# Writing out the order of all five engine queues in a scan, gated MLP and mixture-of-experts kernel

## Chip, core and metric

The kernel runs on one core of one Trainium2 chip. The metric is the device time of one execution in microseconds (us); the time before is the median of three runs.

The core has a matrix engine (PE, whose weight loads the profile lists apart as PEld), a vector engine (DVE), an activation engine (ACT), a general engine (POOL) and a queue engine (SP) that issues the loads. Each works through its own list of instructions in order, and waits where an instruction needs a result of another engine.

## The reference, cut to what matters

Three stages run one after the other. All inputs are float32 when drawn; the two matrices of the second stage reach the kernel as 64-bit floats.

```python
# 1. scan: 4 x 8 heads, 768 positions, head width 32, state 16
L = np.exp(cum[..., :, None] - cum[..., None, :]) * causal
y_intra = (C @ B.T * L) @ x
y_inter = (C @ state) * np.exp(cum)
state = decay * state + (B * decay_from_j).T @ x
# 2. MLP over x of 3072 tokens x 256
h = x @ w_in                                   # 256 -> 2048
x = (h * (1 / (1 + np.exp(-1.702 * h)))) @ w_out   # 2048 -> 256
# 3. eight experts, one for each token
expert_idx = np.argmax(normalised(x) @ normalised(expert_emb).T / tau, axis=1)
out[mask] = gate_w[mask, None] * (np.maximum(x[mask] @ w1[e], 0.0) @ w2[e])   # 256 -> 1024 -> 256
```

## The kernel before, in words

**Tiles and groups.** The 3072 tokens are 24 tiles of 128, and three tiles make a group of 384 (`TPG`, `NG` = 8). The scan handles a tile as two chunks of 64 positions, in four stages: `ssm_a` (lines 282 to 294) scales x into `xtb` on POOL; `ssm_c` (311 to 338) makes the state update `pU` on PE, and on DVE the carried state `T` and its decayed copy `S`; `ssm_b` (296 to 309) makes the score matrix `pS` on PE and masks it into `mt` on DVE; `ssm_d` (340 to 371) makes `pY` on PE from `mt` and `S`, scales it on DVE (`ye`), and splits it into a high part on ACT (`yh`) and a low part on POOL (`yl`). Two heads lie side by side in a matmul, with zeros kept in `c4b` and `xtb` where heads must not mix.

**MLP blocks.** A block (g, f) takes a group g through one of 16 slices f of the hidden width: `gemm1` (line 440) makes six matmuls of 384 columns into `ph`, ACT applies the gate twice (445, 446), DVE forms the low part (447), and `gemm2` (456), two blocks later, makes nine matmuls of 256 columns. There are 128 blocks. Groups 0 and 1 make the first pass together (32 blocks), groups 2 to 7 one pass each. The first pass also decodes the weights: `decode_w` (254 to 275) turns each of 16 slices of 64-bit words into two 32-bit parts, with three ACT operations, three on DVE (266, 268, 272) and two on POOL (270, 275). A block needs its slice decoded.

**Experts.** After a group's pass its tokens are routed (`route0` to `route3`; the expert products are 24 DVE operations at line 515 for groups 0 to 5, and go through PE transposes for 6 and 7) and scattered by expert into `slots`. Ten expert units then run the third stage (`egemm1`, line 657, and `egemm2`, 683).

**What sets the order.** Up to the expert units only SP's queue is in the written order; the program is also written in some order for the other engines, but there a scheduler chooses, instruction by instruction, which ready one comes next. From the expert units on, all are in written order. The loads go out by the table `LOADS`: three buffers hold scan inputs, `c4b` is refilled in place, and the edge factors `ee` come back from memory after a round trip through `ebuf`. An instruction at the head of SP's queue that waits for a buffer holds up every load behind it.

```python
SEQ = ("t0 t1 t2 t3 t4 t5 d0 d1 d2 d3", "")
LOADS = ("s0 c0 s1 s2 w0", "c1 e0 e1", "s3 w1", "s4 w2", "s5 w3", "", "", "")
MENG = {mybir.EngineType.SP}
    man.enter_context(tc.manual_schedule(engines=MENG))
```

Of the kernel before, what the change touches and what calls it, by code (L numbers as in the profile page):

```python
# [24 lines left out]
P = 128  # L25
# [11 lines left out]
DLEAD = 4  # L37
GDOT = 6
NXT = 2
LAG = 1  # L40
TSW = 6
SEQ = ("t0 t1 t2 t3 t4 t5 d0 d1 d2 d3", "")
EORD = (1, 0)
XV = ((), ())
YV = ()
LV = ()
LOADS = ("s0 c0 s1 s2 w0", "c1 e0 e1", "s3 w1", "s4 w2", "s5 w3", "", "", "")
FH = 4
MENG = {mybir.EngineType.SP}
SOFF = (1, 2, 3, 4)  # L50
ROFF = (8, 9, 4, 5)
# [8 lines left out]
SB2, SBT, SX = 256, 256, 256  # L60
SSMW = SB2 + SBT + SX

K_TRI, K_SEL, K_MASK, K_ID, K_RANK, K_ONE, K_W8, K_EB, K_E8, K_PK, K_NK, K_BK, K_CAP, K_END = (
    0, 128, 160, 224, 352, 480, 608, 616, 624, 632, 640, 664, 688, 696)
NBLK = 24


def host_constants():
# [16 lines left out]
    c[:, K_CAP:K_CAP + NE] = CAPS  # L85
    tok = (np.arange(NTILE)[None, :] * P + i[:, None]).astype(np.int32)
# [3 lines left out]
def host_layout(x, a, B, C):  # L90
# [16 lines left out]
    ct = C.reshape(NB, NH, TPB, P, NS).transpose(0, 2, 1, 4, 3).reshape(NTILE, P, P)  # L107
    at = a.reshape(NB, 2, 4, TPB // TPG, TPG, P).transpose(5, 0, 3, 2, 4, 1).reshape(P, -1)
# [15 lines left out]
def body(ctx, tc, ssm, ct, aall, cst, tok, wcat, emb, tau, w1, w2, out):  # L124
# [20 lines left out]

    NGB = 4
# [14 lines left out]
    man.enter_context(tc.manual_schedule(engines=MENG))  # L161
# [8 lines left out]

    warm = const.tile([P, 1], F32, name="warm")
# [3 lines left out]
    c4b = [sp.tile([P, NPAIR, TPG, P], F32, tag=f"c4{i}", name=f"c4b{i}", bufs=1) for i in range(2)]  # L175
    xtb = [sp.tile([P, 2, NPAIR, 2, HD], F32, tag=f"xt{i}", name=f"xtb{i}", bufs=1) for i in range(NXT)]
    nc.vector.memset(c4b[0], 0.0)
    for xt in xtb:
        nc.gpsimd.memset(xt, 0.0)
    nc.vector.memset(c4b[1], 0.0)  # L180

    raw_s, c4_s, ee_s = {}, {}, {}

    def load_c4(g):
        c4_s[g] = c4b[g % 2]
        for p in range(NPAIR):
            h = slice(32 * p, 32 * p + 32)
            nc.sync.dma_start(out=c4_s[g][h, p, :, :],
                              in_=ct[g * TPG:(g + 1) * TPG, h, :].rearrange("t p c -> p t c"))
# [8 lines left out]
    def load_ssm(t):  # L198
        r = sp.tile([P, SSMW], F32, tag="raw", name=f"raw{t}", bufs=3)
        nc.sync.dma_start(out=r, in_=ssm[t])  # L200
        raw_s[t] = r

# [6 lines left out]
    loads = {"s": load_ssm, "c": load_c4, "e": load_ee, "w": load_w}  # L209

    def load(names):
        for n in names.split():
            loads[n[0]](int(n[1:]))

    load(LOADS[0])
# [824 lines left out]
```

## Time and profile before

| | |
|---|---|
| median of three runs | 604.48 us (604.26 to 604.73) |
| the profiled execution | 605.19 us |
| its span, first to last instruction | 603.4 us |
| mean granted clock of PE | 0.97 of full speed |
| busy | PE 553.6 us (92%), DVE 352.1 (58%), ACT 249.6 (41%), POOL 180.2 (30%) |
| on the chain that ended last | PE 68%, issue 9%, DVE 9%, DMA 7%, ACT 3% |

The profiled execution is 0.7 us above the median, and 1.8 us of its time lie outside the span. A share over the whole span is a mean over stages with different limits, so the stages are read apart. PE's records are pipelined: two records that follow each other overlap, and what one costs is read from start to start, not from its own length. A float32 matmul of the scan is recorded as two passes, a matmul of the MLP or the experts as one.

### The profile page before, as it was taken

What the parts mean: (1) busy time and instruction counts of PE and PEld (TensorE: products, weight loads), DVE (VectorE), ACT (ScalarE), POOL (GpSimd) and SP (SyncE); (2) the same over time, 40 slices, a digit from 0 to 9 for tenths busy, and PEclk for the clock granted to TensorE, in tenths of its full rate; (3) what the DMA queues carried; (4) which work ended last, traced back from release to release, by engine and by line L of the source; (5) the groups of instructions that cost most, each with busy time, mean ns of one, the idle gap of its engine ahead of it and who ended that gap; (6) DMA issues with size and microseconds to landing.
All of it is one profiled execution on the core that took longest, in us unless ns stands there. A gap on an engine that the chain in (4) does not pass through costs nothing.

```text
span 603.4 us, 11521 instructions
## 1 busy us (share of the span) xinstructions
PE 553.6 (92%) x4318; PEld 510.4 (85%) x4318; DVE 352.1 (58%) x1019; ACT 249.6 (41%) x578; POOL 180.2 (30%) x204
## 2 busy tenths in 40 slices
PE   5487678999999999999999999998999999999992
PEld 3256568899899889999898999997999999999992
DVE  3284699723796862863762862446576865545330
ACT  3152566533533433433433433448355445445220
POOL 4382588700113421122222202039221102211111
PEclk9688888999999999999999999999999999999996
DMA  6616769401003112011101000057146534231000
GB/s 193 168 66 172 252 211 276 136 27 54 1 2 93 53 36 81 30 36 55 57 7 48 2 1 28 2 167 266 66 150 212 186 117 153 101 106 45 25 25 24
DMA packets 32759, 56.27 MB, mean 93 GB/s; under 512 B 3306, under 2 KB 22592, under 8 KB 32576
## 3 DMA queue, kind: packets, MB, share of 16 engines
q1 hardware_dynamic: 30208, 49.22, 26.7%
q0 software_dynamic: 2496, 6.32, 2.9%
q8 instruction: 34, 0.56, 0.4%
q14 instruction: 21, 0.17, 0.1%
HBM read 44.87 MB, written 11.01 MB: 93 GB/s over the span
## 4 chain that ended last, share of the span: by engine, by line
PE 68%; issue 9%; DVE 9%; DMA 7%; ACT 3%; POOL 1%; SPq 1%; POOLq 0%; ACTq 0%; DVEq 0%
PE ph L440 20%; PE po L456 16%; PE qo L683 9%; PE qh L657 9%; PE po_a L456 3%; PE pS L304 3%; PE pY L350 2%; DMA raw<-in_ssm 2%; DMA wraw<-in_wcat 2%; PE pY L358 2%; PE pU L318 2%; POOL out L129 1%; DVE u L266 1%; DVE glb L447 1%; DVE S L331 1%
## 5 line engine op out<-in xcount | busy, mean ns | idle before, releaser
L440 PE MATMUL ph<-yh,dw 128*128 128x384 f32 x512 | 164.4, 362 | 10.6 <-DVE glb L447 8.7
L445 ACT ACTIVATE ghb<-ph 128x384 fp32r<-128x384 f32 x128 | 62.8, 491 | 172.4 <-PE ph L440 171.0
L447 DVE TENSOR_TENSOR glb<-ph,ghb 128x384 fp32r<-128x384 f32 x128 | 70.9, 554 | 104.0 <-ACT ph L446 101.5
L440 PEld LDWEIGHTS ph<-yh,dw 128*128 128x128 f32 x512 | 95.8, 191 | 19.9 <-DVE glb L447 11.1
L456 PE MATMUL po<-dw,ghb 128*128 128x256 f32 x576 | 104.0, 286 | 1.4 <-ACT ghb L445 1.4
L440 PE MATMUL ph<-yl,dw 128*128 128x384 f32 x256 | 87.1, 340 | 0.0
L456 PEld LDWEIGHTS po<-dw,ghb 128*128 128x128 f32 x576 | 84.2, 189 | 2.9 <-ACT ghb L445 1.6
L456 PE MATMUL po<-dw,glb 128*128 128x256 f32 x288 | 68.7, 282 | 1.1 <-DVE glb L447 1.1
L129 POOL DMA_INDIRECT out<-ob,xs x29 | 29.2, 1006 | 127.2 <-DVE ob L694 121.2
L290 POOL TENSOR_TENSOR xtb<-raw,einv 64x256 f32<-64x256 f32 x48 | 33.3, 694 | 104.5 <-PE pY L350 61.4
L446 ACT ACTIVATE ph<-ph 128x384 f32<-128x384 f32 x128 | 62.5, 488 | 0.0
L664 DVE SCALAR_TENSOR_TENSOR glb<-qh,ghb 128x256 fp32r<-128x256 f32 (+5 forms) x72 | 36.4, 507 | 41.8 <-ACT ghb L663 38.5
L515 DVE SCALAR_TENSOR_TENSOR pr<-xr,enb 128x256 f32<-128x256 f32 x144 | 59.3, 451 | 0.1
L683 PE MATMUL qo<-weh,ghb 128*128 128x256 f32 x208 | 58.6, 282 | 0.0
L683 PE MATMUL qo<-wel,ghb 128*128 128x256 f32 x208 | 58.5, 281 | 0.0
L683 PE MATMUL qo<-weh,glb 128*128 128x256 f32 x208 | 58.5, 281 | 0.0
L663 ACT ACTIVATE ghb<-qh 128x256 fp32r<-128x256 f32 (+5 forms) x72 | 32.5, 452 | 61.6 <-PE qh L657 57.8
L657 PE MATMUL qh<-xh,weh 128*128 128x256 f32 (+5 forms) x160 | 53.3, 333 | 1.8 <-DVE glb L664 1.1
L657 PE MATMUL qh<-xl,weh 128*128 128x256 f32 (+5 forms) x160 | 51.4, 321 | 0.1
L657 PE MATMUL qh<-xh,wel 128*128 128x256 f32 (+5 forms) x160 | 51.2, 320 | 0.0
L456 PEld LDWEIGHTS po<-dw,glb 128*128 128x128 f32 x288 | 49.1, 188 | 1.4 <-DVE glb L447 1.3
L440 PEld LDWEIGHTS ph<-yl,dw 128*128 128x128 f32 x256 | 49.3, 193 | 0.3
(179 smaller groups left out, 1016.9 us busy)
## 6 DMA issues: line engine op xcount, KB each, us to landing
wer<-in_w SPq DMA_DIRECT2D x32, 512.0 KB, 3.6
raw<-in_ssm SPq DMA_DIRECT2D x24, 384.0 KB, 3.0
wraw<-in_wcat SPq DMA_DIRECT2D x16, 512.0 KB, 4.2
slots<-padr SPq DMA_DIRECT2D x8, 516.0 KB, 11.1
ee<-ebuf SPq DMA_DIRECT2D x8, 384.0 KB
xs<-slots SPq DMA_DIRECT2D x3, 516.0 KB
c4b<-in_ct SPq DMA_DIRECT2D x32, 48.0 KB, 4.3
xs<-slots SPq DMA_DIRECT2D x3, 387.0 KB, 3.2
```

The source lines that it names most:

```text
L129: i = nc.gpsimd.indirect_dma_start(in_offset=None, oob_is_err=False, **kw)
L290: eng.tensor_tensor(out=xt[hs, :, :, h, :].rearrange("p c q d -> p (c q) d"), in0=r[hs, SB2 + SBT:].rearrange("p (c d) -> p c d", d=HD), i ...
L440: nc.tensor.matmul(ph, lhsT=wslice(w, f, k * P, k * P + P), rhs=y[g][:, k, :], start=(n == 0), stop=(n == 5))
L445: nc.scalar.activation(out=a[:, :GT], in_=ph, func=AF.Gelu_apprx_sigmoid)
L446: nc.scalar.activation(out=ph, in_=ph, func=AF.Gelu_apprx_sigmoid)
L447: nc.vector.tensor_tensor(out=c[:, :GT], in0=ph, in1=a[:, :GT].bitcast(F32), op=ALU.subtract)
L456: nc.tensor.matmul(po[g][tl], lhsT=l, rhs=r, start=(f == 0 and i == 0 and (off + tl) % 2 == 0), stop=(f == NF - 1 and i == 2), skip_group_ ...
L515: nc.vector.scalar_tensor_tensor(out=pr, in0=xr[:, tl, :D], scalar=1.0, in1=enb[:, e, :], op0=ALU.mult, op1=ALU.mult, accum_out=ld[:, tl, ...
L657: nc.tensor.matmul(ph[:, :n], lhsT=w[:, o:o + P], rhs=x[u][:, k, :n], start=(i == 0), stop=(i == 5))
L663: nc.scalar.activation(out=a[:, :n], in_=ph[:, :n], func=AF.Relu)
L664: nc.vector.scalar_tensor_tensor(out=c[:, :n], in0=ph[:, :n], scalar=0.0, in1=a[:, :n].bitcast(F32), op0=ALU.max, op1=ALU.subtract)
L683: nc.tensor.matmul(qacc(u, s), lhsT=l, rhs=r, start=(f == 0 and i == 0 and (s % 2 == 0 or ss is not None)), stop=(f == NFE - 1 and i == 2) ...
```

## The change

It does five things.

1. All engines are in written order from the start. The start and the first pass follow the string `START`, in which a letter is one operation (on one engine, or one run on PE) and the number the tile, weight slice or block: A scales x, U, S and Y are PE runs of the scan, T, M, E, s, H and L its steps on DVE, ACT and POOL; R, u, p, v, h and l are the steps of `decode_w`; G, g, c and O are `gemm1`, the gate, the low part and `gemm2`; N and W are loads. The later passes are lists of jobs with a block number each.
2. The scan's matmuls no longer carry zeros for the other head: they use 32 or 64 rows and 32 output columns at a place of their own in PE's array. A tile has 8 (U), 4 (S) and up to 32 (Y) matmuls where it had 8, 2, 8 and 4. In the later passes U and S stand together as one run, and Y is a second run two blocks later. DVE makes the carried state in one operation instead of two, and the decayed copies move to ACT (four small operations a tile). POOL scales x in one operation instead of two.
3. Scan inputs have six buffers instead of three, C comes with them (512 KB a tile) and `c4b` with its loads is gone. Groups 0 and 1 take their edge factors from PE (24 small matmuls a group) instead of through memory. Six tiles and five weight slices are asked for at the start.
4. The first two weight slices have their low part made on DVE instead of POOL.
5. Routing is spread over a pass: DVE operations two or three to a block, the rest in steps; group 1 is routed through PE instead of with 24 DVE operations. The order of the experts is settled after six groups instead of seven, and the first experts' weights are loaded and split from block 4 of the last pass.

The core of the diff:

```diff
-SEQ = ("t0 t1 t2 t3 t4 t5 d0 d1 d2 d3", "")
-LOADS = ("s0 c0 s1 s2 w0", "c1 e0 e1", "s3 w1", "s4 w2", "s5 w3", "", "", "")
+PEG = (1, 6, 7)
+NXT = 3
+START = (
+    "A0 X0 A1 U0 A2 x0 T0 S0 s0 U1 M0 R0 u0 S1 Y0 T1 W5 p0 M1 s1 U2 E0 S2 A3 T2 H0 Y1 r4 R1 u1 U3 E1 L0 s2 W6 r0 "
+    "M2 p1 H1 T3 Y2 s3 v0 S3 E2 L1 R2 M3 X1 A4 h0 u2 H2 U4 x1 l0 S4 W7 N6 N7 N8 T4 p2 Y3 M4 s4 v1 E3 L2 h1 Y4 H3 "
+    "v2 R3 l1 G0 E4 A5 h2 L3 U5 g0 T5 S5 l2 H4 G1 c0 s5 M5 L4 g1 Y5 u3 R4 O0 c1 W8 p3 E5 G2 H5 v3 O1 r1 g2 L5 h3 "
...
-    man.enter_context(tc.manual_schedule(engines=MENG))
+    man.enter_context(tc.manual_schedule(engines={mybir.EngineType.SP, mybir.EngineType.PE, mybir.EngineType.DVE,
+                                                  mybir.EngineType.Activation, mybir.EngineType.Pool}))
...
-        r = sp.tile([P, SSMW], F32, tag="raw", name=f"raw{t}", bufs=3)
+        r = sp.tile([P, SSMW], F32, tag="raw", name=f"raw{t}", bufs=6)
...
+    for t in range(3):
+        load_ssm(t)
+    load_w(0)
+    load_ssm(3)
+    load_w(1)
+    load_ssm(4)
+    load_ssm(5)
+    for f in (2, 3, 4):
+        load_w(f)
...
     def ssm_b(t):
...
         for c in range(2):
-            nc.tensor.matmul(ps[:, c * 256:(c + 1) * 256], lhsT=r[:, c * P:(c + 1) * P],
-                             rhs=c4_s[g][:, :, tl, c * Q:(c + 1) * Q], start=True, stop=True)
+            for w in range(2):
+                h = slice(64 * w, 64 * w + 64)
+                nc.tensor.matmul(ps[:, w, c * P:(c + 1) * P].rearrange("p (k i) -> p k i", k=2),
+                                 lhsT=r[h, c * P:(c + 1) * P], rhs=cpad(t)[h, :, c, :],
+                                 start=(c == 0), stop=True, skip_group_check=True)
...
+    def ssm_state(t):
...
+                nc.vector.scalar_tensor_tensor(out=T, in0=old, scalar=dec[:, i:i + 1], in1=u, op0=ALU.mult, op1=ALU.add)
...
+    def ssm_pads(t):
+        for s1, old, i in st[t]["pads"]:
+            for r in range(2):
+                nc.scalar.mul(out=s1[:, r, :], in_=old, mul=decm[:, i, r:r + 1])
...
     def ssm_d(t):
...
+        def place(k, q, r, c):
+            o = 32 * (2 * q + (k ^ r))
+            return py[o:o + 32, r, c * Q:(c + 1) * Q]
+
+        heads = [(k, q, r) for q in range(2) for k in range(2) for r in range(2)]
         for c in range(2):
...
+            for k, q, r in heads:
+                h = slice(64 * r, 64 * r + 64)
+                nc.tensor.matmul(place(k, q, r, c), lhsT=xt[h, c, 2 * k + q, :], rhs=mt[h, k, c, q, :],
+                                 start=(c == 0), stop=True, skip_group_check=True)
...
+            for k, q, r in heads:
+                h = slice(32 * (2 * k + q), 32 * (2 * k + q) + 32)
+                nc.tensor.matmul(place(k, q, r, c), lhsT=sps[c][h, r, :], rhs=cpad(t)[h, q, c, :],
+                                 start=False, stop=True, skip_group_check=True)
...
+    seq0 = [(0, f) for f in range(LEAD)] + [(1, 0)]
+    for f in range(1, NF):
+        seq0 += [(1, f)] + ([(0, f + LEAD - 1)] if f + LEAD - 1 < NF else [])
...
+    def tile_steps(jobs, t0, at):
+        for i, k in enumerate(at):
+            for d, w in ((0, "U"), (0, "T"), (2, "Y"), (3, "E")):
+                jobs.append((k + d, lambda t=t0 + i, w=w: step(t, w)))
```

SP's queue at the start, before (`raw` is a tile's scan input, `wraw` a weight slice):

```order
L166 DMA al<-in_aall 128x576
L167 DMA kc<-in_cst 128x696
L200 DMA raw_111<-in_ssm 128x768
L188 DMA c4b_103<-in_ct 32x3x128 x4
L207 DMA wraw_121<-in_wcat 128x512
L229 DMA ebuf<-et 96x2x128
L188 DMA c4b_104<-in_ct 32x3x128 x4
L194 DMA ee_155<-ebuf 128x1x768
L200 DMA raw_198<-in_ssm 128x768
L207 DMA wraw_200<-in_wcat 128x512
```

and now:

```order
L184 DMA al<-in_aall 128x576
L185 DMA kc<-in_cst 128x698
L207 DMA raw_112<-in_ssm 128x1024
L217 DMA wraw_118<-in_wcat 128x512
L207 DMA raw_120<-in_ssm 128x1024
L217 DMA wraw_122<-in_wcat 128x512
L217 DMA wraw_302<-in_wcat 128x512
L286 DMA ebuf<-et 96x2x128
```

The write of `et` and the reads of `ebuf`, which wait for ACT and for each other, stood ahead of the fourth tile and the second weight slice; now twelve loads stand ahead of the write (of those alike, some are left out in both lists), and the first read of `ebuf` comes later still.

DVE's queue, now, from the first tile's state to what the first MLP block waits for (`u` and `v` are steps of the decode, `dw` its result):

```order
L395 COPY T_0_236<-pU_224 128x32
L369 TENSOR_TENSOR mt_257<-pS_241,kc 128x512
L316 TENSOR_SCALAR u_263<-wraw_118 128x512
L318 SCALAR_TENSOR_TENSOR u_263<-wraw_118,u_263 128x512
L403 SCALAR_TENSOR_TENSOR T_0_297<-T_1_239,dec,pU_248 128x32
L444 TENSOR_TENSOR ye_322<-pY_271,ee_234 128x256
L327 SCALAR_TENSOR_TENSOR v_451<-ab_261,u_263 128x512
L336 TENSOR_TENSOR dw_0_173<-v_451,dw_0_169 128x512
L369 TENSOR_TENSOR mt_563<-pS_510,kc 128x512
```

Steps of tiles and of weight slices alternate; rows of the same kinds between these are left out. The first three slices' `u` stand ahead of the first block now, where the second stood behind a load that came late.

PE's queue in a later pass, one tile, before (each row but the last two with some sixteen MLP matmuls behind it):

```order
L318 MATMUL pU_1496<-xtb_106,raw_1438 32x64 x2
L318 MATMUL pU_1496<-xtb_106,raw_1438 32x64 x6
L350 MATMUL pY_1582<-mt_1553,xtb_106 64x64 x4
L358 MATMUL pY_1582<-c4b_104,S_0_1505 64x2x64 x2
L358 MATMUL pY_1582<-c4b_104,S_1_1509 64x2x64 x2
```

and now, with two blocks between the second row and the third:

```order
L381 MATMUL pU_1763<-xtb_109,raw_1539 32x32 x8
L361 MATMUL pS_1772<-raw_1539 128x128 x4
L426 MATMUL pY_1852<-mt_1787,xtb_109 32x64 x16
L433 MATMUL pY_1852<-raw_1539,S_0_1777 32x64 x8
L433 MATMUL pY_1852<-raw_1539,S_1_1780 32x64 x8
```

The six pieces of a tile (the score matrix and a second piece of L350 stand elsewhere in the list of before) have become two, and the matmuls of a tile 44 instead of 22.

## Rows read from the trace of the kernel before

**Rows 1.** Busy time by stage: us, then PE, PEld, DVE, ACT, POOL, clock, DMA.

```profile
0.00:60.00 60.00, 39.12 (x346) 29.23 (x347) 29.83 (x62) 20.01 (x39) 27.48 (x46) 0.86 0.55 149
60.00:112.00 52.00, 41.05 (x315) 36.27 (x313) 46.13 (x63) 31.18 (x62) 37.95 (x30) 0.90 0.81 240
112.00:158.10 46.10, 44.49 (x338) 41.36 (x338) 19.09 (x48) 18.71 (x47) 9.42 (x12) 1.00 0.14 44
158.10:419.80 261.70, 258.52 (x2072) 238.16 (x2073) 159.09 (x626) 105.99 (x268) 69.72 (x84) 1.00 0.16 53
419.80:603.40 183.60, 170.40 (x1253) 165.41 (x1251) 97.92 (x223) 73.74 (x163) 35.65 (x35) 0.98 0.31 103
```

**Rows 2.** The chain that ended last, in order of time: start, us, what.

```profile
14.01 14.33 DMA raw<-in_ssm
...
52.78 12.11 DMA wraw<-in_wcat
```

**Rows 3.** PE's timeline, one block with nothing between: start, us, line and matmul.

```profile
397.90 0.34 PE L440 MATMUL ph<-yh,dw 128*128 128x384 f32 x1
...
398.94 0.28 PE L456 MATMUL po<-dw,glb 128*128 128x256 f32 x1
...
400.01 0.34 PE L440 MATMUL ph<-yh,dw 128*128 128x384 f32 x1
```

**Rows 4.** Groups of matmuls between 158.1 and 419.8 us: count, busy us, mean ns.

```profile
L440 PE MATMUL ph<-yh,dw 128*128 128x384 f32 x368 | 116.4, 357 | 1.4 <-DVE glb L447 1.4
L456 PE MATMUL po<-dw,ghb 128*128 128x256 f32 x576 | 104.0, 286 | 1.4 <-ACT ghb L445 1.4
...
L318 PE MATMUL pU<-xtb,raw 128*32 128x64 f32 x192 | 10.6, 230 | 0.0
```

**Rows 5.** PE's timeline where parts of the scan stand between blocks.

```profile
17.76 0.43 PE L318 MATMUL pU<-xtb,raw 128*32 128x64 f32 x16
18.12 0.44 PE L358 MATMUL pY<-c4b,S 128*64 128x128 f32 x4
...
120.38 0.44 PE L440 MATMUL ph<-yh,dw 128*128 128x384 f32 x1
...
122.69 0.45 PE L350 MATMUL pY<-mt,xtb 128*64 128x64 f32 x8
123.07 0.44 PE L440 MATMUL ph<-yh,dw 128*128 128x384 f32 x1
...
136.06 1.02 PE L304 MATMUL pS<-c4b,raw 128*128 128x256 f32 x4
136.73 0.53 PE L440 MATMUL ph<-yh,dw 128*128 128x384 f32 x1
```

**Rows 6.** Weight loads of line 318: count, shortest, median and longest ns.

```profile
L318 PEld LDWEIGHTS pU<-xtb,raw x384: 106/109/178, 11.9 to 349.1; 128*32 128x32 f32 x192
```

**Rows 7.** The first step of the decode on DVE: as rows 6, first and last start.

```profile
L266 DVE TENSOR_SCALAR u<-wraw x16: 415/575/1559, 12.4 to 109.2; 128x512 int32<-128x512 int32 x16
```

**Rows 8.** Groups by line over the whole span: count, busy us, mean ns, idle before.

```profile
L447 DVE TENSOR_TENSOR glb<-ph,ghb 128x384 fp32r<-128x384 f32 x128 | 70.9, 554 | 104.0 <-ACT ph L446 101.5 <-ACT ghb L445 1.8 <-issue 0.2
...
L270 POOL TENSOR_TENSOR u<-u,rd 128x512 int32<-128x512 int32 x16 | 23.2, 1452 | 11.0 <-DVE u L268 8.5 <-ACT rd L264 2.4
...
L272 DVE SCALAR_TENSOR_TENSOR v<-ab,u 128x512 f32<-128x512 f32 x16 | 17.8, 1111 | 0.0
...
L307 DVE TENSOR_TENSOR mt<-pS,kc 128x512 f32<-128x512 f32 x24 | 16.5, 686 | 6.2 <-PE pS L304 5.8 <-issue 0.4
L268 DVE SCALAR_TENSOR_TENSOR u<-wraw,u 128x512 int32<-128x512 int32 x16 | 15.1, 946 | 0.2
L266 DVE TENSOR_SCALAR u<-wraw 128x512 int32<-128x512 int32 x16 | 13.2, 822 | 20.0 <-DMA wraw<-in_wcat 19.7
...
L364 DVE TENSOR_TENSOR ye<-pY,ee 128x256 f32<-128x256 f32 x24 | 10.0, 417 | 7.6 <-DMA ee<-ebuf 4.3 <-PE pY L358 2.4 <-POOL yl L369 0.6
...
L336 DVE TENSOR_TENSOR T<-pU,S 128x64 f32<-128x64 f32 x40 | 8.7, 218 | 1.7 <-PE pU L318 1.3
```

More of the change, by code (lines that the diff above doesn't have):

```diff
@@ L173, in body @@
     nc.scalar.activation(out=warm, in_=warm, func=AF.Ln)
[L175 to L189, printed above, removed]
+    xtb = [sp.tile([P, 2, NPAIR, HD], F32, tag=f"xt{i}", name=f"xtb{i}", bufs=1) for i in range(NXT)]
+    raw_s, ee_s = {}, {}
     def load_ee(g):
@@ L426, in prefill, with router3 @@
+    def router3():
+        pen = pss.tile([P, 512], F32, tag="m", name="pen")
+        for k in range(2):
+            nc.tensor.transpose(pen[:, k * NE:(k + 1) * NE], em[:, k * P:(k + 1) * P], ident[:NE, :NE])
+        nc.vector.tensor_copy(out=ent.rearrange("p k e -> p (k e)"), in_=pen[:, :2 * NE])
     def prefill(e):
@@ L434, in gemm1 @@
     def gemm1(g, f):
[L435 removed]
+        pf = hbank()
         ph = pf[:, :GT]
@@ L722, in rows_of, with early_rows @@
         return rreg[k]
+    early_base = const.tile([P, NE], F32, name="early_base")
+    def early_rows():
+        nc.vector.tensor_tensor(out=base, in0=base, in1=early_base, op=ALU.max)
     def expert_order():
@@ L839, in body, with tile_loads @@
+    for n in START.split():
+        fns[n[0]](int(n[1:]))
+    def tile_steps(jobs, t0, at):
+        for i, k in enumerate(at):
+            for d, w in ((0, "U"), (0, "T"), (2, "Y"), (3, "E")):
+                jobs.append((k + d, lambda t=t0 + i, w=w: step(t, w)))
+    def tile_loads(jobs, t0, at):
+        for i in range(TPG):
+            jobs.append((at + 2 * i, lambda t=t0 + i: load_ssm(t)))
+    order, first = expert_order(), set()
     for pi, gs in enumerate(passes):
         jobs = []
-        nxt = passes[pi + 1] if pi + 1 < len(passes) else ()
@@ L868, in body @@
+        if gn < NG:
+            tile_steps(jobs, TPG * gn, (2, 6, 10))
+        if gn + 1 < NG:
+            tile_loads(jobs, TPG * (gn + 1), 7)
+            jobs += [(13, lambda t=TPG * (gn + 1) + i: step(t, "A")) for i in range(TPG)]
+            jobs.append((14, lambda: load_ee(gn + 1)))
         if pi + 1 == len(passes):
@@ L887, in body @@
                 po[gs[0]] = [pts[0][:, :D], pts[0][:, D:], pts[1][:, :D]]
-            for i, g in enumerate(gs):
-                lag = LAG * i
-                for ff in range(f - lag if f >= lag else NF, f - lag + 1 if f < NF - 1 else NF):
-                    block(g, ff)
-            for ff, fn in jobs:
-                if ff == f:
+            block(g, ff)
+            for k, fn in jobs:
+                if k == f and fn in first:
+                    fn()
+            low_part()
+            for k, fn in jobs:
+                if k == f and fn not in first:
                     fn()
@@ L954, in body @@
         finish(NU - 1, [s])
-    hand.close()
     man.close()
```

460 lines of the change are left out of this document (249 added, 211 removed), and 8 rows, old and new, of the table START.

## The prediction, made before the changed kernel was run

> **What bounds the kernel now.** I read the stages first, because the share of PE over the whole span hides them. From 158.1 to 419.8 us PE is busy for 258.5 of 261.7 us at a granted clock of 1.00, and the experts behind it keep PE at 170.4 of 183.6 [rows 1]: there PE is the bound, and only less work on PE can help. The two stages ahead of 112 us are different. PE is busy for 39.1 of 60 and 41.1 of 52 us there, at 0.86 and 0.90 of its clock [rows 1], and in the second DVE is busy for 46.1 of 52. The chain of waits says what came last: a scan load of 14.3 us and then a weight load of 12.1 us [rows 2]. These are loads that were issued late, behind others on SP's queue; DVE stood idle for 19.7 us before the decode's first step with a weight load as the releaser [rows 8]. After the second load DVE had the decode of the remaining slices in front of it, all at once. So the start is bound by loads, then by DVE, and everything behind it by PE.
>
> **Prices.** A block without anything between takes 1.04 us for its six matmuls and 1.07 us for its nine, 2.11 us from start to start [rows 3]. A run of scan passes in the middle costs more than its passes: a block with eight passes of line 350 inside takes 2.69 us (120.38 to 123.07), 0.58 more, while these passes themselves take 0.38 (122.69 to 123.07) [rows 5]. So changing from MLP matmuls to scan and back costs about 0.2 us each time.
>
> **Scan tiles in the later passes.** Of the 258.5 busy microseconds, 368/4 = 92 runs of six matmuls (95.7 us) and 576/6 = 96 runs of nine (102.7) are MLP [rows 1, 4], which leaves 60 for 192/16 = 12 tiles [rows 4] and the routing. Priced by the timeline, a tile's `pU` takes 0.36 us, `pS` 0.67 (136.06 to 136.73), its sixteen passes of line 350 twice 0.38 [rows 5]; its eight of line 358, twice as wide, I put at 0.8, and six switches at 1.2. That is 3.8, or 46 for twelve, and with slowed neighbours (which I can't part from routing) somewhat over 4 each; the rest, some 7 to 10 us, is routing.
>
> After the change a tile is two runs (0.4 us of switches). `pU` has the same sixteen passes: 0.36. `pS` has eight passes of half the width where four took 0.67: 0.4 to 0.8, and I keep 0.67. `pY` is the uncertain term: 32 matmuls, 64 passes of 64 columns into 32 array columns each. The nearest row is `pU`, whose passes also go to 32 array columns and stream 64 columns: sixteen in 0.36 us, 22.5 ns each. The other end is line 350, whose passes take 64 array columns: 0.38/8 = 47 ns [rows 5]. That makes 1.44 to 3.0 us. I take `pU`'s, because what is alike is the placing, and get 0.36 + 0.67 + 1.44 + 0.4 = **2.9 us** a tile, with 2.6 to 4.6 as the ends. DVE's state operations of 218 ns [rows 8] are halved; their copies go to ACT, which is busy for 106 of 261.7 us [rows 1], and hide there.
>
> **The start.** With the loads asked for up front, DVE has work from 12.4 us, when the first weight slice is there [rows 7]. The new queue puts onto DVE, ahead of what the first block needs: three `u` steps (3 × (0.822 + 0.946) = 5.3), eight state operations (8 × 0.22 = 1.8), four masks (4 × 0.69 = 2.7), three `ye` (3 × 0.42 = 1.25), one `v` (1.11) [rows 8], and the first low part, for which I take the mask's 0.69 as the same size of tile. Together 12.9 us, so 25.3; then `Y4` on PE and its hand-over, 2 to 3 us. First block at about **28 us**.
>
> **The first pass.** Each of 16 slices brings two blocks and a quarter of a tile (tiles 5 to 8). PE: 2 × 2.11 + 2.9/4 = 4.95 us. DVE: 0.822 + 0.946 + 1.111 for the decode, two `glb` of 0.554, and a quarter of a tile's two state operations, mask and `ye`, (2 × 0.218 + 0.686 + 0.417)/4 = 0.39: 4.4 us [rows 8]. PE is the longer, but the two hand work to each other many times per slice and neither may now overtake; I add 5% and take 5.2. 16 × 5.2 = 83, so the first pass ends at 28 + 83 = **111 us**, with two groups through the MLP and nine tiles scanned.
>
> **The rest.** 96 blocks × 2.11 = 202.6; 15 tiles × 2.9 = 43.5; routing 9 (the 7 above and 2 for group 1, now on PE); idle 3, as now [rows 1]. That is 258, so the experts begin at 369 and not at 419.8. They and the tail are unchanged: 183.6 [rows 1]. Span 369 + 184 = 553; with the 1.8 us outside the span 555, against 605.2 of the profiled execution. The execution stands 0.7 above the median, so 554.5: I say **555 us**, some 50 less, of which about 33 come from the start and 17 from the tiles.
>
> **Set to nothing, with the cover.** The larger scan loads (512 KB a tile) go through DMA engines that are busy 0.81 at the most now and 0.16 later [rows 1]; if they came late again, the stall of 12 to 14 us [rows 2] would be back. ACT's added copies lie beside 31.2 busy of 52 us [rows 1]. The 24 edge matmuls a group, 48 passes at 22.5 ns and more, are a little over 1 us where PE waits for DVE anyway. The low parts moved to DVE for two slices are in the sum above once; the second costs 0.7 of DVE's slack. Later loads pass nothing that blocks on SP's queue, since six buffers replace three.
>
> **Rival 1: DVE and POOL get in each other's way.** The first decode step took from 415 to 1559 ns for one shape, median 575 [rows 7], and POOL's step of the same decode takes 1452 ns [rows 8]: the slow ones are as long as if DVE stood still for one operation of POOL. If in the tight first pass all three decode steps last 1.56, DVE needs 3 × 1.56 + 2 × 0.554 + 0.39 = 6.2 us a slice, 16 × 6.2 = 99, the pass ends at 127 and the kernel at **571**. For it: POOL has almost 3 us of decode per slice, two steps of that size. Against: my means already hold the mixture, much of it from a stage with POOL busy for 38 of 52 us [rows 1]. Chance 0.18. [...]
>
> **Rival 2: the small passes of `pY` wait for their weights (slower).** A weight load of `pU` takes 106 ns [rows 6], longer than a small pass. The two passes of a float32 matmul use the same rows of the array, so if a load can't run beside a pass on its own rows, 32 of `pY`'s 64 loads wait, and 8 more where line 433 uses the same rows for neighbouring matmuls: 40 × (0.106 − 0.0225) = 3.3 us a tile. Fifteen tiles cost 50 more, the five that the first pass and the start feel 17: **622**, slower by 17; with all 64 loads waiting it would be 662. It decides where the gain of 50 us is used up, at 2.5 us a tile, 30 loads that wait. Against it stands `pU`, which starts a pass every 22.5 ns [rows 5], all on the same full set of rows, while its loads are recorded at 106 [rows 6]. Chance 0.06. [...]
>
> **Rival 3: the written order is no better than the scheduler's.** If the start gave nothing, because a new wait in a queue that may no longer be overtaken took the place of the load stalls, the tiles' 17 us alone would remain: **588**. The rows of the change show that the earlier loads and the two-run tiles are there, so this needs a new stall of 33 us. Chance 0.02.
>
> **How the numbers follow.** My case has 0.74. The low end takes the first block at 26 us with PE's own 4.95 per slice (a pass end at 105), the tile at 2.6, and no idle: 555 − 6 − 4.5 − 3 = 541. The high end takes a tile of 4.6 (15 × 1.7 = 26, so 581) or Rival 1 with 0.4 us a tile besides, and holds Rival 1: 582. Rivals 2 and 3 lie outside, and what of my own case goes wrong in two terms at once, together under 0.2. A measurement here can tell 0.2% from no change, 1.2 us. Faster is 0.92, which leaves out of my case, Rival 1 and Rival 3 (0.94 together) 0.02 for an unforeseen wait; that goes half to no change, 0.01, and half to slower, with Rival 2 0.07.
>
> **What would show it.** Right: the first `gemm1` matmul near 28 us; group 1's last block near 111; no load on the chain of waits after 15 us; a granted clock of 1.00 from soon after the first block; passes of `pY` 22 to 31 ns from start to start; PE over 95% busy from 111 us to the experts. Wrong: runs of `pY` of 4 us and more (Rival 2); decode steps on DVE with means over 1.3 us and PE waiting for DVE through the first pass (Rival 1); PE idle behind a wait of DVE or ACT for something late in its own list (Rival 3).

## The result, and the profile after

The changed kernel takes 543.94 us (543.18 to 544.93, 4 runs) against 604.61 us (604.26 to 606.29, 4 runs) in the same comparison: a ratio of 0.8993 with a 95% interval of [0.897, 0.9016]. That is some 61 us less, inside the predicted range and 11 us below its point. All ratios leave out slow runs; in the comparison of the experiments e9 and e10 below these are two of seven runs of the kernel before (762 and 1036 us).

The stages of the changed kernel, cut at its own marks (first block, end of the first pass, start of the experts' second product); columns as in [rows 1]:

```profile
0.00:27.84 27.84, 18.82 (x535) 14.24 (x535) 14.42 (x35) 15.96 (x41) 13.42 (x37) 0.88 0.88 324
27.84:112.00 84.16, 80.88 (x846) 76.00 (x838) 51.18 (x107) 58.68 (x135) 44.72 (x42) 1.00 0.57 174
112.00:357.60 245.60, 242.12 (x2832) 232.07 (x2833) 160.74 (x577) 122.03 (x335) 59.38 (x69) 0.99 0.19 65
357.60:541.40 183.80, 168.84 (x1241) 163.82 (x1239) 97.26 (x220) 73.06 (x161) 32.78 (x33) 0.98 0.29 96
```

Against [rows 1], the stage at the lower clock is now only the start, 27.8 us at 0.88 where 112 us ran at 0.86 and 0.90: behind the first block PE is busy for 80.9 of 84.2 us at full clock, with DVE at 51.2.

Where the time went is seen in three groups of matmuls: `gemm2` of the first pass (`po_a`), `gemm2` of the later passes (`po`) and `gemm1` (`ph`). Their rows give the shortest, median and longest ns, and then the first and the last start. Before:

```profile
L456 PE MATMUL po_a<-dw,ghb x192: 274/282/470, 42.5 to 153.9; 128*128 128x256 f32 x192
L456 PE MATMUL po<-dw,ghb x576: 274/282/472, 159.3 to 419.5; 128*128 128x256 f32 x192
L440 PE MATMUL ph<-yh,dw x512: 334/337/689, 37.6 to 414.7; 128*128 128x384 f32 x171
```

and after:

```profile
L541 PE MATMUL po_a<-dw,ghb x192: 277/282/388, 33.5 to 110.2; 128*128 128x256 f32 x192
L541 PE MATMUL po<-dw,ghb x576: 278/282/415, 111.9 to 355.9; 128*128 128x256 f32 x192
L516 PE MATMUL ph<-yh,dw x512: 334/336/522, 27.8 to 351.7; 128*128 128x384 f32 x171
```

The first block starts at 27.8 us instead of 37.6, the first pass ends at 110.2 instead of 153.9, and the later passes take 355.9 − 110.2 = 245.7 us instead of 265.6. So of the 62.0 us by which the span is shorter (541.4 against 603.4), 43.7 lie up to the end of the first pass and 19.9 in the later passes; what follows takes 1.6 more.

One scan tile on PE's timeline, the rows of MLP matmuls between the two runs left out:

```profile
113.13 0.33 PE L381 MATMUL pU<-xtb,raw 128*32 128x32 f32 x16
113.39 0.71 PE L361 MATMUL pS<-raw 64*128 64x128 f32 x8
114.04 0.44 PE L516 MATMUL ph<-yh,dw 128*128 128x384 f32 x1
...
119.12 0.46 PE L426 MATMUL pY<-mt,xtb 64*32 64x64 f32 x32
119.50 0.47 PE L433 MATMUL pY<-raw,S 32*32 32x64 f32 x32
119.90 0.44 PE L516 MATMUL ph<-yh,dw 128*128 128x384 f32 x1
```

From start to start `pU` takes 0.26 us, `pS` 0.65, and `pY`'s 64 passes 0.78, that is 12 ns a pass in the mean.

And DVE's steps of the decode, which answer to the three rows of [rows 8]:

```profile
L318 DVE SCALAR_TENSOR_TENSOR u<-wraw,u 128x512 int32<-128x512 int32 x16 | 12.5, 779 | 0.5
L327 DVE SCALAR_TENSOR_TENSOR v<-ab,u 128x512 f32<-128x512 f32 x16 | 11.5, 718 | 2.3 <-POOL u L323 2.3
L316 DVE TENSOR_SCALAR u<-wraw 128x512 int32<-128x512 int32 x16 | 7.3, 458 | 0.6 <-DMA wraw<-in_wcat 0.6
```

The same operations on the same data take 1.96 us a slice now, where they took 2.88. The wait for a weight load went from 19.7 us to 0.6.

### The profile page after: what moved, and what is told of

It is laid out like the page before. It is cut to its first block, busy times and chain, and to the rows that moved or that the text cites. A ratio compares the mean times of both kernels' runs of the same rounds, so it can differ in the third digit from the quotient of the medians.

```text
span 541.4 us, 13668 instructions
## 1 busy us (share of the span) xinstructions
PE 510.7 (94%) x5440; PEld 486.1 (90%) x5440; DVE 323.6 (60%) x934; ACT 269.7 (50%) x669; POOL 150.3 (28%) x180
## 3 DMA queue, kind: packets, MB, share of 16 engines
q1 hardware_dynamic: 26360, 50.00, 28.1%
## 4 chain that ended last, share of the span: by engine, by line
PE 70%; issue 13%; DVE 6%; ACT 4%; DMA 3%; POOL 2%; SPq 0%; POOLq 0%; ACTq 0%; DVEq 0%
PE ph L516 23%; PE po L541 16%; PE ph L741 8%; PE qo L767 7%; PE po_a L541 7%; PE pS L361 2%; POOL out L138 2%; DMA wraw<-in_wcat 2%; PE pY L433 1%; PE pY L426 1%; DVE glb L533 1%; ACT ph L526 1%; PE pU L381 1%; ACT ghb L525 1%; PE pX L727 1%
## 5 line engine op out<-in xcount | busy, mean ns | idle before, releaser
L516 PE MATMUL ph<-yh,dw 128*128 128x384 f32 x512 | 156.3, 346 | 3.4 <-DVE glb L533 3.0
L541 PEld LDWEIGHTS po<-dw,ghb 128*128 128x128 f32 x576 | 94.1, 190 | 0.6 <-ACT xr L554 0.6
L541 PE MATMUL po<-dw,glb 128*128 128x256 f32 x288 | 81.4, 283 | 0.0
L747 ACT ACTIVATE ghb<-ph 128x256 fp32r<-128x256 f32 (+5 forms) x72 | 32.6, 452 | 62.1 <-PE ph L741 62.1
L748 DVE SCALAR_TENSOR_TENSOR glb<-ph,ghb 128x256 fp32r<-128x256 f32 (+5 forms) x72 | 36.5, 508 | 42.2 <-ACT ghb L747 42.0
L741 PE MATMUL ph<-xh,weh 128*128 128x256 f32 (+5 forms) x160 | 53.1, 332 | 3.3 <-DVE glb L748 2.6
L693 DVE TENSOR_TENSOR wel<-wer,weh 128x512 fp32r<-128x512 f32 x56 | 45.4, 810 | 12.0 <-ACT weh L692 10.9
L741 PE MATMUL ph<-xl,weh 128*128 128x256 f32 (+5 forms) x160 | 51.4, 322 | 0.1
L741 PE MATMUL ph<-xh,wel 128*128 128x256 f32 (+5 forms) x160 | 51.2, 320 | 0.0
L454 POOL TENSOR_TENSOR yl<-ye,yh 128x256 fp32r<-128x256 f32 x24 | 20.0, 835 | 106.5 <-ACT yh L449 71.7
```

What stands on the lines that cost most here:

```text
L454: nc.gpsimd.tensor_tensor(out=yl[g][:, :, o:o + P], in0=ye, in1=yh[g][:, :, o:o + P].bitcast(F32), op=ALU.subtract)
L516: nc.tensor.matmul(ph, lhsT=wslice(w, f, k * P, k * P + P), rhs=y[g][:, k, :], start=(n == 0), stop=(n == 5))
L541: nc.tensor.matmul(po[g][tl], lhsT=l, rhs=r, start=(f == 0 and i == 0 and (off + tl) % 2 == 0), stop=(f == NF - 1 and i == 2), skip_group_ ...
L693: eng.tensor_tensor(out=lo[:, o], in0=r, in1=hi[:, o].bitcast(F32), op=ALU.subtract)
L741: nc.tensor.matmul(ph[:, :n], lhsT=w[:, o:o + P], rhs=x[u][:, k, :n], start=(i == 0), stop=(i == 5))
L747: nc.scalar.activation(out=a[:, :n], in_=ph[:, :n], func=AF.Relu)
```

## Experiments: which of the five parts did it

Two runs take one part of the change back each. The first gives the order of four queues back to the scheduler and keeps tiles, loads and routing; the experts stay in written order (`hand`).

```diff
-    man.enter_context(tc.manual_schedule(engines={mybir.EngineType.SP, mybir.EngineType.PE, mybir.EngineType.DVE,
-                                                  mybir.EngineType.Activation, mybir.EngineType.Pool}))
+    man.enter_context(tc.manual_schedule(engines={mybir.EngineType.SP}))
...
+    hand = ExitStack()
+    hand.enter_context(tc.manual_schedule(engines={mybir.EngineType.PE, mybir.EngineType.Activation,
+                                                   mybir.EngineType.DVE, mybir.EngineType.Pool}))
```

> The changed kernel, in which up to the experts only SP's queue keeps the written order and the scheduler chooses the order of the other four, as before the change; tiles, loads and routing stay as changed. Theory (the written order is what shortened the first pass, from 154 us before to 110 us): the later passes keep most of their gain, the first pass ends 15 to 40 us later than at 110 us, and the time is 560 to 585 us. Rival (the early loads and the packed tiles alone did it): the first pass ends by 113 us and the time is 543 to 549 us.

Measured: 601.71 us, ratio 0.9973 [0.996, 0.9986]. Nearly the whole gain is gone, more than the theory's 560 to 585 us had asked for.

```profile
L540 PE MATMUL po_a<-dw,ghb x192: 274/282/553, 58.3 to 160.3; 128*128 128x256 f32 x192
L540 PE MATMUL po<-dw,ghb x576: 277/282/415, 164.2 to 416.1; 128*128 128x256 f32 x192
L515 PE MATMUL ph<-yh,dw x512: 334/336/689, 42.2 to 412.7; 128*128 128x384 f32 x171
```

The first block comes at 42.2 us, later than before the change, and the first pass ends at 160.3. The later passes take 255.8 us: what e1 keeps (the packed tiles, and with them the loads and the routing) is worth about 10 us there, and the written order the other 10. DVE's rows of this run (view by line, whole span) and a piece of its timeline show how:

```profile
L317 DVE SCALAR_TENSOR_TENSOR u<-wraw,u 128x512 int32<-128x512 int32 x16 | 21.3, 1329 | 0.3
L326 DVE SCALAR_TENSOR_TENSOR v<-ab,u 128x512 f32<-128x512 f32 x16 | 17.7, 1107 | 2.1 <-POOL u L322 2.1
L315 DVE TENSOR_SCALAR u<-wraw 128x512 int32<-128x512 int32 x16 | 15.6, 977 | 2.3 <-DMA wraw<-in_wcat 2.0
```

```profile
33.52 1.43 DVE L326 SCALAR_TENSOR_TENSOR v<-ab,u 128x512 f32<-128x512 f32 x1
34.99 0.72 DVE L315 TENSOR_SCALAR u<-wraw 128x512 int32<-128x512 int32 x1
...
35.74 1.75 DVE L317 SCALAR_TENSOR_TENSOR u<-wraw,u 128x512 int32<-128x512 int32 x1
...
38.98 0.41 DVE L443 TENSOR_TENSOR ye<-pY,ee 128x256 f32<-128x256 f32 x1
```

Before the first block DVE has begun the decode of eight slices here (eight `u` steps from 11.26 to 40.52 us), in the changed kernel of three. A tile's `ye`, on which PE waits, stands behind them, and from 28 to 60 us DVE is busy for 31.5 of 32 us. And the three steps take 3.41 us a slice instead of 1.96, 23 us over 16 slices. With the loads early more slices are ready early, and the scheduler has more of them to put first; that fits a first block 4.6 us later than before the change, though early loads under the old order were not run apart.

The second run takes back the early requests: three buffers, and the loads of tiles 3 to 5 and slices 1 to 4, with those behind them, ordered where a buffer comes free.

```diff
-        r = sp.tile([P, SSMW], F32, tag="raw", name=f"raw{t}", bufs=6)
+        r = sp.tile([P, SSMW], F32, tag="raw", name=f"raw{t}", bufs=3)
...
-    load_ssm(3)
-    load_w(1)
...
+    ("... Y0 N3 W1 T1 ... Y1 N4 W2 ... Y2 N5 W3 W4 W5 W6 ... Y3 N6 ... Y4 N7 ... Y5 N8 ...")
```

> The changed kernel with three buffers for scan inputs instead of six and with the loads of the tiles 3 to 5 and of the weight slices 1 to 4 asked for only when a buffer is free, one after the other as before the change; all other queues as changed. Theory (the load stalls of 14.3 and 12.1 us were what the early loads took away): the stalls come back, 15 to 27 us more, 559 to 571 us. Rival (in the written order tiles release their buffers so early that a late load costs only what DVE stands still for): the weight slice 1 lands about 5 us after DVE asks for it, 2 to 8 us more, 546 to 552 us.

Measured: 543.35 us, ratio 0.9016 [0.8997, 0.9035], the same as the changed kernel. DVE does wait for slice 1, and it does not matter:

```profile
17.85 0.47 DVE L310 TENSOR_SCALAR u<-wraw 128x512 int32<-128x512 int32 x1 [2.46 <-DMA wraw<-in_wcat]
```

The first block comes at 28.0 us and the first pass ends at 110.1. The theory falls, and the rival's 2 to 8 us were still too much: with the order written, neither six buffers nor early requests are needed.

This run does not make the loads as late as they were before. Slice 1 reaches DVE at 17.85 us here; in the kernel before it was this:

```profile
29.64 0.43 DVE L266 TENSOR_SCALAR u<-wraw 128x512 int32<-128x512 int32 x1 [6.46 <-DMA wraw<-in_wcat]
```

and SP's queue had waited there, in the first 60 us, mainly for these three:

```profile
SPq L200 <- PE pU L318: 15.9, 2, 12.6
SPq L408 <- DVE em L406: 13.2, 1, 13.2
SPq L194 <- DMA ebuf<-et: 2.8, 1, 2.8
```

These are the buffer of a tile still at work, the expert embeddings that a late step on DVE had to make ready, and the round trip of the edge factors. The load of 14.3 us [rows 2] went out behind the last of them, that of 12.1 us behind the second. e2 puts back the first kind only (up to 60 us SP waits for it 21.9 us in all), and it costs nothing.

## Experiments: which queue's order

Three more runs keep the order written on some engines and leave the others to the scheduler; the edit is that of e1 with other sets of engines.

> The changed kernel with the written order kept on DVE (and SP) alone; the scheduler chooses for PE, ACT and POOL up to the experts. With all four free (e1) the first block began at 42 us and the first pass ended at 160, DVE was busy for 31.5 of the 32 us from 28 to 60, mostly with the decode of slices that no block could use yet, while masks and scaling of tiles waited. Theory (DVE's order is what the scheduler gets wrong): the first block begins by 31 us, the first pass ends by 122 us, and with the later passes between 246 us (two runs a tile) and 256 us (as in e1) the time is 543 to 565 us. Rival (PE's own order decides): the first pass ends after 140 us, 573 us or more.

> The changed kernel with the written order kept on PE (and SP) alone; the scheduler chooses for DVE, ACT and POOL up to the experts. Theory (DVE's order decides the first pass, PE's the later ones): the first pass ends after 140 us as in e1, or later since PE may not overtake what waits for DVE, the later passes take 244 to 249 us, 575 to 605 us in all. Rival (PE's own order decides): the first pass ends by 122 us, 543 to 558 us.

> The changed kernel with the written order on DVE, POOL (and SP); the scheduler chooses for PE and ACT up to the experts. With DVE alone written (e9) the first pass ended at 126.9 us, with a PE wait of 5.2 us for POOL's scaling of x. Theory (POOL's order is the rest of the first pass, and PE's order only splits the tiles into more runs): the first pass ends by 116 us and the later passes take 249 to 256 us, 548 to 557 us. Rival (the rest lies in PE's and ACT's order): the first pass ends after 121 us, 557 to 566 us.

Measured, with the runs around them; the times are medians, the marks are read from the same three groups of matmuls as above, and the last column is from the end of the first pass to the last start of `po`:

| written besides SP | time, us | ratio to before, 95% interval | first block | first pass ends | later passes |
|---|---|---|---|---|---|
| none (e1) | 601.71 | 0.9973 [0.996, 0.9986] | 42.2 | 160.3 | 255.8 |
| PE (e10) | 581.37 | 0.963 [0.9589, 0.9671] | 50.5 | 147.6 | 247.9 |
| DVE (e9) | 563.45 | 0.9316 [0.9273, 0.9359] | 28.1 | 126.9 | 250.6 |
| DVE, POOL (e12) | 557.32 | 0.9236 [0.9201, 0.9271] | 28.6 | 117.9 | 251.4 |
| all (the change) | 543.94 | 0.8993 [0.897, 0.9016] | 27.8 | 110.2 | 245.7 |

The granted clock of the first 112 us goes along with it: 0.76, 0.74, 0.88, 0.95 and 0.97 down the table, so the marks hold what the clock costs too: in the kernel before, matmuls of `ph` start 0.32 us apart at a granted clock of 0.50 (65.5 to 67.5 us), and 0.17 at 1.00 [rows 1, 3].

DVE's order alone brings the first block to where the change has it and the first pass to 126.9 us; that is 4.9 us past what the theory allowed, while its time is inside. With PE's order alone, as its theory had it, the first pass ends after 140 us and the later passes gain; the first block comes later than with none, since PE now stands behind what DVE has not done. PE's longest waits in e10 up to 150 us, and one of those in e9:

```profile
PE pY L425 <- DVE ye L443: 16.1, 3, 8.6
PE pY L425 <- DVE mt L368: 6.5, 1, 6.5
```

```profile
PE pU L380 <- POOL xtb L348: 6.2, 2, 5.2
```

In e9 the longest wait has moved to POOL's scaling of x, and with POOL written too (e12) the pass ends 9 us earlier; the forecast of 116 us was missed by 2 and the time lies at the edge of both. The last 8 us of the first pass take PE's and ACT's order as well. In the later passes PE's order alone takes 7.9 us off (255.8 to 247.9), DVE's alone 5.2. So each queue gives a part, and DVE's the largest, 33 of the 50 us between e1 and the change in the first pass.

To see what the place of the decode alone does, one run moves a piece of the written start. Nothing is added.

```diff
-    "... s2 W6 r0 M2 p1 H1 T3 Y2 s3 v0 S3 ..."
+    "... s2 W6 r0 p1 v0 h0 l0 R2 u2 v1 h1 l1 p2 R3 u3 v2 h2 l2 p3 v3 h3 l3 M2 H1 T3 Y2 s3 S3 ..."
```

> The changed kernel with one piece of the written start moved: the rest of the decode of the weight slices 0 to 3 (all steps after the first, on DVE, ACT and POOL) stands ahead of tile 2's mask and tile 3's state, as in the order that the scheduler chose in e1; all queues stay in written order and nothing is added. The first block needs slice 0 and tiles 0 to 2, so the decode of the slices 1 to 3 is early work for DVE and POOL. Theory (the first pass starts late because DVE decodes ahead of the tiles, and beside a busy POOL): the first block begins 6 to 12 us after 27.8 us, the decode steps of slices 1 to 3 are longer than with the changed order, and the work saved later does not come back since PE bounds the first pass: 549 to 557 us. Rival (DVE's work is the same in sum, so the first pass catches up): first block later, but the first pass ends within 2 us of 110.3 us, 543 to 546 us.

Measured: 554.41 us, ratio 0.9191 [0.9163, 0.9219]. The first block comes at 40.6 us, 12.8 later and a little more than the theory's 12; the first pass ends at 121.3, and the later passes take the same 245.8. So 11 of the 12.8 us are never made up; the rival falls. One part of the theory falls too: DVE's steps are not longer here (in the first 40 us the second takes 0.79 us and the third 0.69 in the mean, in the change 0.97 and 0.69). DVE stands still, at the head of a queue that nothing may overtake, and PE with it:

```profile
PE pY L428 <- DVE T L405: 12.9, 1, 12.9
```

```profile
20.69 0.69 DVE L338 TENSOR_TENSOR dw<-v,dw 128x512 fp32r<-128x512 f32 x1 [2.93 <-ACT dw L334]
...
29.62 0.69 DVE L329 SCALAR_TENSOR_TENSOR v<-ab,u 128x512 f32<-128x512 f32 x1 [3.24 <-POOL u L325]
```

So the place of the decode costs time here by another way than in e1, where DVE was busy almost without a pause; this run does not show e1's. A written order is worth as much as its places are right: one wrong piece costs 10 us of the 61.

## Experiments: the price of a tile

Two runs put the matmuls of `pY` in other orders; a third splits each tile of the later passes into four runs on PE.

```diff
-        heads = [(k, q, r) for q in range(2) for k in range(2) for r in range(2)]
+        heads = [(k, q, (k ^ w)) for q in range(2) for w in range(2) for k in range(2)]
```

> The changed kernel with the matmuls of pY in another order: neighbours use the same 32 columns of PE's array and different rows. In the change neighbours use different columns, and each half of pY (32 passes, on line 426 or 433) takes 0.39 us from start to start. Theory (passes run beside each other where their columns of the array differ): the halves take 0.6 to 1.2 us. Rival (only different rows let a weight load run beside a pass): they stay at 0.35 to 0.45 us.

```diff
-        heads = [(k, q, r) for q in range(2) for k in range(2) for r in range(2)]
+        heads = [(k, q, r) for r in range(2) for q in range(2) for k in range(2)]
```

> The changed kernel with the matmuls of pY in a third order: on line 426 four neighbours use the same 64 rows and four different sets of columns, on line 433 four neighbours use four different sets of rows and of columns. Theory (columns decide): both halves stay at 0.35 to 0.45 us. Rival (a load waits where the rows are the same): line 426 takes 24 more waits of 0.084 us, about 2.4 us, and line 433 stays at 0.39 us or below.

PE's timeline of e5 and then of e6:

```profile
119.76 0.46 PE L426 MATMUL pY<-mt,xtb 64*32 64x64 f32 x32
120.14 0.47 PE L433 MATMUL pY<-raw,S 32*32 32x64 f32 x32
120.55 0.44 PE L516 MATMUL ph<-yh,dw 128*128 128x384 f32 x1
```

```profile
26.49 0.46 PE L426 MATMUL pY<-mt,xtb 64*32 64x64 f32 x32 [0.81 <-DVE ye L444]
26.88 0.47 PE L433 MATMUL pY<-raw,S 32*32 32x64 f32 x32
27.27 0.45 PE L516 MATMUL ph<-yh,dw 128*128 128x384 f32 x1
```

Each half takes 0.38 to 0.41 us in every order. That leaves neither rule standing by itself, the one on columns in e5 nor the one on rows in e6: among these orders the neighbours do not matter. No order puts two matmuls with the same rows and the same columns side by side, so a rule that wants both is not tested, and what lets the passes follow each other in 12 ns in the mean is not settled. (The times, 543.76 and 542.68 us from one execution each, say no more.)

The third edit, where u, s, y and Y are the four runs, t the state and m the mask:

```diff
...
-            for d, w in ((0, "U"), (0, "T"), (2, "Y"), (3, "E")):
+            for d, w in ((0, "u"), (0, "t"), (1, "s"), (1, "m"), (2, "y"), (3, "Y"), (4, "E")):
```

> The changed kernel with each tile of the later passes in four runs on PE instead of two: pU, pS, and the two halves of pY one block apart each. Theory (each change from MLP matmuls to scan and back costs about 0.2 us): 2 more a tile, 15 tiles, 6 us more, 548.5 to 551.5 us. Rival (the weight loads of the next run hide the change, and the cost lies in the passes): within 1.2 us of the changed kernel, 543 to 545 us.

Measured: 546.93 us, ratio 0.9071 [0.9036, 0.9106], against 0.8993. The later passes take 361.5 − 110.3 = 251.2 us, 5.5 more than 245.7, for 30 more changes between MLP and scan: 0.18 us each, close to the 0.2 of the prediction. The median moved by 3 us only, below the expected 548.5; what follows the later passes took 183.9 us in this profile against 185.5 in that of the change.

## Experiments: POOL and DVE, and a wait in the written order

> The changed kernel with the low parts of the first two experts' weights all on DVE instead of every second one on POOL, in the last pass. In the profile of the change PE stood still for 3.0 us at 341.5 us, behind a low part on DVE that took 6.25 us beside five on POOL in a row (6.26 us). Theory (DVE was shut out while POOL worked): each low part on DVE takes 0.67 to 0.75 us, PE's stall is gone, 540 to 542 us. Rival (the weights came late, as the chain of waits has a load of 3.44 us there): the stall stays within 0.5 us of 3.0 us, 543 to 546 us.

```diff
-                    e, w, q, i, nc.gpsimd if k % 2 else nc.vector)))
+                    e, w, q, i, nc.vector)))
```

What the edit aims at, in the profile of the change, on DVE, POOL and PE's list of waits:

```profile
337.74 6.25 DVE L693 TENSOR_TENSOR wel<-wer,weh 128x512 fp32r<-128x512 f32 x1
```

```profile
337.18 6.26 POOL L693 TENSOR_TENSOR wel<-wer,weh 128x512 fp32r<-128x512 f32 x5
```

```profile
PE ph L516 <- DVE glb L533: 3.0, 1, 3.0
```

Three scatters had held POOL up (333.45 to 337.16 us), so five low parts stood ready and ran without a gap; DVE's own, started in between, ended only after the fifth (343.99 against 343.44 us). With all of them on DVE:

```profile
L693 DVE TENSOR_TENSOR wel<-wer,weh x64: 677/685/693, 333.2 to 489.4; 128x512 fp32r<-128x512 f32 x64
```

The longest of 64 takes 693 ns, the stall of 3.0 us is gone, with the loads in the same order, and `po` ends at 352.7 us instead of 355.9, in spite of a first pass that ended 0.3 later. In the change DVE was held over five operations of POOL, not one: its 0.69 us became 6.25 beside their 6.26. By what, the trace does not show. The time is 540.96 us, ratio 0.8981 [0.8949, 0.9012]; by the runs alone that is not told apart from the change's 0.8993 [0.897, 0.9016], the 3 us are read from the trace. Its median is the lowest measured here.

> The changed kernel with the low part of all 16 weight slices on DVE (0.68 us each) instead of 14 on POOL (1.3 us each). Theory (POOL's work slows DVE's operations with two inputs from SBUF, but PE bounds the first pass): the second and third decode step on DVE come down from 0.78 and 0.72 to 0.69 us or a little above, DVE has 9.6 us less of slack in the first pass, and the time stays within 1.5 us, 542.5 to 545.5 us. Rival (DVE is as good as the bound of the first pass, as its 4.4 of 4.95 us a slice in the prediction had it): DVE's 0.6 us more a slice come out on PE, 5 to 9 us more, 549 to 553 us.

```diff
-    LV = (0, 1)
+    LV = tuple(range(NF))
```

Measured: 545.25 us, ratio 0.9034 [0.9004, 0.9064]; the first pass ends at 110.6 us. PE bounds it, as the theory had it, and DVE's slack takes the rest. The other half of the theory was too simple:

```profile
L336 DVE TENSOR_TENSOR dw<-v,dw x16: 678/1414/1608, 23.1 to 98.0; 128x512 fp32r<-128x512 f32 x16
```

The second decode step came down from 779 to 718 ns, the third did not (734 against 718), and the moved step itself took 1414 ns in the median where 684 were expected: it now stands beside POOL's remaining step, and ends some 0.55 us after it:

```profile
59.55 1.59 DVE L336 TENSOR_TENSOR dw<-v,dw 128x512 fp32r<-128x512 f32 x1
```

```profile
59.31 1.28 POOL L323 TENSOR_TENSOR u<-u,rd 128x512 int32<-128x512 int32 x1 [1.93 <-DVE u L318]
```

The long step moved with the work, from the second (779 to 718 ns) to the one that left POOL (1414).

> The changed kernel with the four matmuls and the ACT step that make the edge factors for the round trip through memory (r4) behind the edge factors of group 1 (x1), some 8 us later. In the profile of the change ACT stood still for 3.0 us at that step, and behind it the state copies of tile 2, for which DVE waited 2.0 and PE 1.1 us. Theory (a written order costs where an engine must wait at the head of its queue): the first block starts 1.5 to 3 us before 27.8 us, 541 to 542.5 us. Rival (DVE's own work sets the first block, and ACT's wait is cover): first block within 0.5 us of 27.8 us, 543.3 to 544.5 us.

```diff
-    "... H0 Y1 r4 R1 ... U4 x1 l0 ..."
+    "... H0 Y1 R1 ... U4 x1 r4 l0 ..."
```

Measured: 546.57 us, ratio 0.9057 [0.9034, 0.9081], and the first block at 29.5 us, later by 1.7: both expectations fall. ACT's stop only moved (it waited 4.1 us for group 1's edge factors), and in those PE stopped for 2.21 us between equal matmuls:

```profile
19.54 1.27 PE L268 MATMUL pee<-kc,al 128*32 128x128 f32 x17
23.03 0.97 PE L268 MATMUL pee<-kc,al 128*32 128x128 f32 x28 [2.21 <-issue]
```

The granted clock from 20 to 36 us, behind and around the stop, is 0.65 in this profile against 0.89 in that of the change. The profile names nothing that PE waited for, so this run does not tell theory from rival, and the cause of the stop stays open.

## Why the prediction was right, and where it was not

**The start and the first pass** came out to a microsecond: the first block at 27.8 us (28 predicted), a slice in (110.2 − 27.8)/16 = 5.15 us (5.2), the end at 110.2 (111). PE bounds the pass (busy for 80.9 of 84.2 us), as forecast. The DVE price behind it was too high: 1.96 us a slice for the decode steps, not 2.88, so DVE needs about 3.5 and not 4.4 us a slice. In the start the shorter steps were paid back by waits that the sum did not have (DVE 2.0 us for ACT's state copies). Both points are so close partly by luck: with the tile at its measured 2.1 us (below) PE's own work is 4.75 us a slice and not 4.95, so waits and other work took 0.4 us and not the 0.25 of the 5%. Of the other signs, PE's share behind 112 us (242.1 of 245.6 us) came as said, and no load after 11.4 us is on the chain up to 112 us; SP's queue does still wait for buffers, once for 32.6 us, which was said not to happen, and it costs nothing.

**The step that failed** is "so the start is bound by loads", as the owner of the 33 us. The loads were late before and stood on the chain [rows 2]. But e1 keeps every load of the change, DVE waits 2.0 us for weights there, and the first block still comes at 42.2 us, because DVE takes the decode first. With DVE's order written (e9) it comes at 28.1 us, and with all orders written and later requests (e2) at 28.0. So in the changed kernel the order in which DVE takes its work sets the start, and the early requests do nothing that shows. The chain had shown which load came last, and not what SP's queue stood behind: a buffer, the edge factors and a step on DVE. What the late loads cost the kernel before under its own order, and whether the written order would do as much with the edge factors still going through memory, no run shows. So the sum was right with the wrong owner: the 33 us put down to the start are, like about half of the later passes' gain (10 of 20), had only with the written order. For the same reason Rival 3's price was wrong: with an order no better than the scheduler's the tiles' 17 us do not remain; at most 2.4 us do (603.16 × (1 − 0.996), by the lower end of e1's interval and the time before in its comparison).

**The term that was mis-sized** is the tile. Of the later passes' 245.7 us, against 258 predicted, 96 blocks of 2.11 us take 202.6 as forecast, and 3.3 are waits (predicted 3, though it is another wait, the 3.0 us of e3). A tile is 0.26 + 0.65 + 0.78 and two changes of 0.2, 2.1 us and not 2.9: 15 × 0.8 = 12 us, the whole of the 12 by which the later passes came out shorter. What is left, 245.7 − 202.6 − 3.3 − 31.5 = 8.3, is routing and the first expert matmuls (predicted 9). `pY` was priced at `pU`'s old 22.5 ns a pass; it takes 12, and `pU` itself, with 32 columns instead of 64, 16. The low end of the tile's bounds, 2.6, was no bound: it was the nearest row itself, and that row is a mean over a run of 16 passes. The trace of before also has shorter runs of `pU`, at the same full clock:

```profile
117.49 0.31 PE L318 MATMUL pU<-xtb,raw 128*32 128x64 f32 x4
117.73 0.44 PE L440 MATMUL ph<-yh,dw 128*128 128x384 f32 x1
...
336.69 0.43 PE L318 MATMUL pU<-xtb,raw 128*32 128x64 f32 x16
337.05 0.34 PE L350 MATMUL pY<-mt,xtb 128*64 128x64 f32 x4
```

Four passes take 0.24 us and sixteen 0.36, so most of a run's time is a fixed part and a further pass costs some 10 ns. An estimate from these rows for 64 passes in one run is 0.36 + 48 × 0.01 = 0.84 us, close to the 0.78 measured, where the mean price gave 1.44.

**The rivals.** Rival 1 did not come in the first pass, where DVE's steps got shorter; in the last pass one DVE operation did take 6.25 us beside POOL, at 3 us of PE, and e1's steps are longer too (3.41 us a slice). Rival 2 did not come at all: passes run at 12 ns in the mean in three orders, in one of them with the same rows for four neighbours. If a load had to wait for a pass on its own rows, 622 us would have come out; for these matmuls the runs show no such wait, with 0.39 us for e6's 32 passes of line 426 where e6's rival had 2.4. The clock came as said, 1.00 from 27.84 to 112 us.

## What to carry to other kernels

A late load at the end of the chain of waits is a symptom until it is shown that an earlier load helps: follow what the queue of loads waits for, a buffer or a step, back to the engine whose order keeps it. Price a pass from two runs of different length, since the mean of a short run holds its fixed part (here 60 ns a pass in a run of four of `pU`, 22.5 in one of sixteen). In a start that is bound by one busy vector engine, put first what the next stage waits for, and work that only becomes ready early (here the decode of slices that no block needs yet) last; a scheduler that takes whatever is ready can do the reverse. In a written order, look for each instruction that waits at the head of its queue, and for POOL operations that can pile up beside a DVE operation: `wel`, with both operands in SBUF, took 6.25 us instead of 0.69 beside five of them, while `glb`, with one in PSUM, took 0.559 at the most in its 128 operations.

## What was not expected of the hardware

- Small float32 passes of 64 columns into 32 columns of the array take 12 ns each in the mean of a run of 32, in three different orders of rows and columns, while the weight loads of `pY` in the changed kernel are recorded at 104 and 107 ns in the median.
- A DVE operation of 0.69 us took 6.25 us beside five operations of POOL in a row (6.26 us) and ended 0.55 us after the fifth.
- PE stopped for 2.21 us between equal matmuls, for nothing that the profile names (e4), and in the 16 us from 20 us on the mean granted clock was 0.65.
